# A recurrent attention and wave-mixing kernel: another order of the work, bf16 weight flips, filler matmuls at the start, and DMA transposes near the end

## The chip, the cores and the metric

One core of a Trainium2 chip runs the kernel: TensorE (PE), VectorE (DVE), ScalarE (ACT), GpSimd (POOL), the queue of SyncE (SP) that issues nearly all DMAs, and 16 DMA engines. The metric is the device time of one execution in microseconds (us). PEld is PE's loading of a stationary operand, which overlaps its matmuls.

## The reference, cut to what matters

Batch 4, 8 heads of 48, 768 tokens, so rows of 384. All inputs and the output are float32.

```python
for t in range(S):                                   # per batch and head
    cur = outer(u * k[t], v[t])
    y[t] = r[t] @ (state + cur)
    state = w[:, None] * state + outer(k[t], v[t])
x = heads of y side by side                          # (B, 768, 384)
theta = x @ w_theta
z = w_tok_r @ (x * cos(theta)) + w_tok_i @ (x * sin(theta))   # over the tokens
u = x + z
out = u + maximum(u @ w_ch, 0)
```

## The kernel before, in words

The recurrence is computed in chunks of 128 tokens: r is scaled by powers of w and k by inverse powers, so that within a chunk the result is a masked product, and between chunks a state is carried. A batch has 6 chunks, taken as 3 pairs (g = 3 x batch + pair, 12 in all). `build` describes the kernel as a list of tasks, in this order of the text:

- `setup` (L308): masks, the identity, and the tables wpow and wpinv of powers of w, which start with a load of w, a matmul on ones (L363) and exponentials on ACT.
- `heads` (L487), per batch: r scaled into Rw (L492), flipped by PE and evacuated as RT, transposed.
- `attention` (L506), per pair: k scaled into Kw (L520, f32 in, bf16 out), flipped as KT; v cast (vb); scores (L543), masked into mAT (L548); the diagonal term (PD L553, L561, dg, yd L568); state sums (L585, L593, L603, L613); outputs (L627, L632), and x (L639). Then x is flipped by PE into a bank (the helper at L473), evacuated as xT, multiplied with w_theta (theta, L651), sine and cosine are taken on ACT (L655, L658), and zr (DVE L661) and zi (POOL L664) are formed.
- `token_weights` (L445): each 128 x 768 block of the two token matrices is loaded in f32, flipped by PE in f32 against an f32 identity (6 transposes, L456, into two banks), and evacuated by ACT or DVE as bf16.
- `mixing` (L668), per pair of chunks of a batch: per chunk 24/2 = 12 matmuls of 384 columns (L683) in four parts of three, which all wait for zr and zi of all three pairs; the sum with x (un, L689); six flips of un (L473) evacuated as uT; six matmuls with w_ch (L700); relu and sum (fin, L704); one store of 384 KB (L708).

The helper `copy` (L257) is the line L259 on ACT and L261 on the others; every load is issued at L404.

`Plan.order` (L88) is a list scheduler that runs when the program is built. Every task carries for each engine that may take it a cost in ns (time on the engine, latency until others see it), data it reads and writes, PSUM banks it needs (two double banks, four single ones), and a priority. It steps through time by these costs, gives each free engine the ready task of the lowest priority number, and so fixes the order on each engine and the engine of each task. At run time every engine goes through its list in that order and waits where an operand is late. Loads have priorities near -1e6 and so go out in the order of the text when their slot (a ring of 10) is free. A `lock` keeps tasks on DVE and POOL that share a port from being planned at the same time. Until `cold` (25 us) the scheduler counts PE's costs 1.6 times.

Of the kernel before, what the change touches and what calls it, by code (L numbers as in the profile page):

```python
# [22 lines left out]
SLOTS = (2, 2, 1, 1, 1, 1)  # L23


class Task:
    __slots__ = ("opts", "fn", "deps", "prio", "seq", "acq", "uses", "nwait", "users", "ready",
                 "start", "done", "end", "mode", "lock", "eng", "name")


class Plan:
# [7 lines left out]
    cold = 25000.0  # L39
# [6 lines left out]
    def add(self, opts, fn, rd=(), wr=(), prio=0.0, acq=(), use=(), mode=0, lock=False, name=""):  # L46
        t = Task()
        t.opts, t.fn, t.prio, t.mode, t.lock, t.name = opts, fn, prio, mode, lock, name
        t.seq = len(self.tasks)
# [24 lines left out]

    def pick_banks(self, acq, free, now, kept):

        got = {}
        avail = [i for i in range(len(self.slots)) if free[i] <= now and i not in kept]
        for tok in sorted(acq, key=lambda k: -self.width[k]):
            c = [i for i in avail if self.slots[i] >= self.width[tok]]  # L80
            if not c:
                return None
            i = min(c, key=lambda i: (self.slots[i], free[i]))
            avail.remove(i)
            got[tok] = i
        return got

    def order(self):  # L88
        for t in self.tasks:
            t.users, t.nwait, t.ready = [], len(t.deps), {e: 0.0 for e in t.opts}  # L90
# [5 lines left out]
        def wake(t):  # L96
            for e in t.opts:
                waiting[e].append(t)
# [11 lines left out]
        while len(out) < n:  # L110
            for e in ENGINES:
                while free_at[e] <= now:
                    best, got = None, None
                    kept = set()
                    for t in sorted(waiting[e], key=lambda t: (t.prio, t.seq)):
                        if t.ready[e] > now or (t.lock and port > now):
                            continue
                        if len(t.opts) > 1:
                            mine = now + t.opts[e][0]
                            if any(max(free_at[o], t.ready[o], now) + t.opts[o][0] < mine  # L120
                                   for o in t.opts if o != e):
# [15 lines left out]
                    for o in t.opts:  # L137
# [5 lines left out]
                    if e == PE:  # L143
                        if t.mode != last_mode:
                            ns += 80.0
                        last_mode = t.mode
                        if now < self.cold:
                            ns *= 1.6
                    if t.lock:
# [39 lines left out]
def act_op(n, psum=True, ptr=False):  # L189
    return (n / 1.2 + (85 if psum else 100) + (90 if ptr else 0), 135)  # L190


def dve_op(n, rate=1.0):
    return (n / (0.96 * rate) + 70, 115)


def pool_op(n, rate=1.8):
    return (170 + rate * n, 100)


def pe_op(ns):
    return (ns, 215)
# [3 lines left out]
def kernel(  # L206
# [15 lines left out]
    ctx.enter_context(tc.manual_schedule())  # L222
    for t in P.order():
# [3 lines left out]
def build(ctx, tc, nc, r, k, v, w, u, moe_w_theta, moe_w_tok_r, moe_w_tok_i, moe_w_ch, out):  # L227
# [39 lines left out]
    pi2 = sb.tile([C, 1], F32, name="pi2")  # L267
    w_row = sb.tile([1, HD], F32, name="w_row")
# [39 lines left out]
    def setup():  # L308
# [6 lines left out]
        def fills(e):  # L315
            nc.vector.memset(ones, 1.0)
# [3 lines left out]
            for t in Sbs:  # L320
                nc.vector.memset(t, 0.0)
# [3 lines left out]
        P.add({DVE: (600, 100)}, fills, wr=["ones", "wu", "pi2", "uw", "bmask", "Sb0"], prio=-200)  # L325
# [81 lines left out]
    def load_r(b, parts=1):  # L407
        n = H // parts
        for i in range(parts):
            h = slice(i * n, (i + 1) * n)  # L410
            load(3500 / parts, r_fs[b % NR][:, h],
# [9 lines left out]
    def load_kv(b, pr, src):  # L421
        i = slot()
        for c in range(2):
            t0 = (2 * pr + c) * C
            load(1080, Ls[i][:, c, :, :D], src[b, :, t0:t0 + C, :].transpose([1, 0, 2]),
# [9 lines left out]
    def square(src, dst, key, prio, pos=None):  # L435
        s3 = src.rearrange("(o p) n -> p o n", p=C)
        for o, n in ((0, 2), (2, 1)):
            i = slot()
            load(560 * n, flat(i)[:, :n * HD].rearrange("p (o c) -> p o c", o=n),
# [5 lines left out]
    def token_weights(tos, prio):  # L445
        for to in tos:
            for src, dst, key in ((moe_w_tok_r, WrT, "WrT"), (moe_w_tok_i, WiT, "WiT")):
                i = slot()
                load(1100, flat(i)[:, :S], src[to * C:(to + 1) * C, :], L2(i))
                tok = ("W", key, to)  # L450

                def flip(e, i=i, tok=tok):
                    for g in range(2):
                        for j in range(3):
                            o = (3 * g + j) * C
                            nc.tensor.matmul(dbl(tok)[:, g, j * C:(j + 1) * C],  # L456
                                             flat(i)[:, o:o + C], ident_f, is_transpose=True,
                                             start=(j == 0), stop=(j == 2))
                P.add({PE: pe_op(660)}, flip, rd=L2(i) + ["ident_f"], acq=[(tok, 2)],
                      prio=prio + to, name="Wflip")  # L460

                def evac(e, tok=tok, dst=dst, to=to):
                    copy(e, dst[:, :, to * C:(to + 1) * C].rearrange("p (g j) c -> p g j c", g=2),
                         dbl(tok)[:, :, :3 * C].rearrange("p g (j c) -> p g j c", j=3))
                P.add({ACT: act_op(6 * C), DVE: dve_op(6 * C)}, evac, use=[tok],
                      wr=[(key, to)], prio=prio + to, name="Wevac")
# [17 lines left out]

    nS = [0]

    def heads(b, base):  # L487

        rf, Rw, RT = r_fs[b % NR], Rws[0], RTs[b % 2]
        for hp in range(HP):  # L490
# [5 lines left out]
            opts = {POOL: pool_op(576, 2.15)}  # L496
            if b == 0:
                opts[DVE] = dve_op(576)
            P.add(opts, scale_r, rd=[("r_f", b % NR, hp)] + [("wpow", n) for n in range(NCH)],
                  wr=[("Rw", hp)], prio=base + 0.1 * hp, lock=True, name="rscale")  # L500
# [5 lines left out]
    def attention(b, pr, base):  # L506
# [16 lines left out]
        opts = {POOL: pool_op(2 * HD, 2.15)}  # L523
        if b == 0:
            opts[DVE] = dve_op(2 * HD)
        P.add(opts, scale_k, rd=L2(ik) + [("wpinv", 0), ("wpinv", 1)], wr=[kK], prio=pb,
              lock=True, name="kscale")
# [3 lines left out]
        P.add({ACT: act_op(2 * HD, False)}, lambda e: copy(  # L531
            e, vb.rearrange("p a (h d) -> p (a h) d", h=H),
            Ls[iv][:, :, :, :D].rearrange("p a h d -> p (a h) d")),
            rd=L2(iv) + ["tables done"], wr=[kv_], prio=pb + 1, name="vcast")

        for c in range(2):
# [18 lines left out]
            rd=[kT] + rt_keys, wr=[kP], prio=pb + 2.5, lock=True, name="PD")  # L555
        td = ("dg", g)

        def diag(e):
# [9 lines left out]
        P.add({POOL: pool_op(2 * HD, 1.7)}, lambda e: nc.gpsimd.tensor_mul(  # L568
            yd.rearrange("p a (h d) -> p (a h) d", h=H), wide(dg, D),
            vb.rearrange("p a (h d) -> p (a h) d", h=H)), rd=[kd, kv_], wr=[ky], prio=pb + 3,  # L570
            lock=True, name="yd")
# [36 lines left out]
        P.add({DVE: dve_op(HD), ACT: (490, 135)}, mid,  # L608
# [10 lines left out]
        def outputs(e):  # L619
            for c in range(2):  # L620
                cc = 2 * pr + c
                first = True
                for s, keep in ((Sb_in, S_in and c == 0), (Sb_mid, c == 1)):
                    if not keep:
                        continue
# [5 lines left out]
                for h in range(H):  # L631
                    nc.tensor.matmul(dbl(ty)[:, c, h * D:(h + 1) * D], mAT[:, c, h % 2, h // 2, :],  # L632
                                     vb[:, c, h * D:(h + 1) * D], start=first,
                                     stop=(h == H - 1), skip_group_check=True)
                    first = False
        P.add({PE: pe_op(740)}, outputs, rd=rt_keys + [kM + (0,), kM + (1,), kv_, S_mid] +
              ([S_in] if S_in else []), acq=[(ty, 2)], prio=pb + 5, name="y")
# [6 lines left out]
        flips(xT, [x[:, 2 * pr + t, dk * C:(dk + 1) * C] for t in range(2) for dk in range(ND)],  # L644
              ("TX", g), pb + 6, xk, [("xT", g % 2)], "xT", ev(6 * C))
        th = ("th", g)

        def theta(e):
# [15 lines left out]
        P.add({POOL: pool_op(2 * HD, 1.9)}, lambda e: nc.gpsimd.tensor_mul(  # L664
            zi[:, 2 * pr:2 * pr + 2], x[:, 2 * pr:2 * pr + 2], sn),
            rd=xk + [("sin", g % 2)], wr=[("zi", zj, pr)], prio=pb + 8, lock=True, name="zi")

    def mixing(b, pr, base):  # L668
        x, zr, zi = xs[b % 2], zrs[b % 2], zis[b % 2]
        zj = b % 2  # L670
        zk = [("zr", zj, o) for o in range(NP)] + [("zi", zj, o) for o in range(NP)]
# [3 lines left out]
        for t in range(2):  # L675
            to = 2 * pr + t
            tm = ("mx", b, to)
            for part in range(4):
                def mix(e, tm=tm, to=to, part=part):
                    WT, z = ((WrT, zr), (WiT, zi))[part // 2]  # L680
                    for j in range(3):
                        so = 3 * (part % 2) + j
                        nc.tensor.matmul(bank(tm)[:, :HD], WT[:, so, to * C:(to + 1) * C],  # L683
                                         z[:, so], start=(part == 0 and j == 0),
                                         stop=(part == 3 and j == 2))
                P.add({PE: pe_op(490)}, mix, rd=zk + [(n, to) for n in ("WrT", "WiT")],
# [77 lines left out]
```

## Time and profile before

| What | us |
|---|---|
| median of three runs (lowest, highest) | 161.48 (159.95, 161.77) |
| the profiled execution | 159.55 |
| its span, from the first to the last instruction | 157.8 |
| busy: PE, DVE, ACT, POOL | 135.1, 110.0, 76.3, 75.6 |
| DMA | 25.00 MB in 59962 packets |

The profile's page gives the busy share of each engine and the same in 40 slices of 3.9 us, each digit a tenth; PEclk is the clock granted to TensorE, in tenths of full speed. Groups of instructions are listed by line, engine and operands with their total and mean time (mean ns of one), and the idle time ahead of them with what ended it. A matmul's own duration includes its way through the array; matmuls overlap, so what one costs is better seen in the chain of work that ended last, which gives a run of them from start to start. A waits row reads: who waited, for whom, us in total, times, longest.

### The profile page before, as it was taken

The page shows a single profiled execution, that of the slowest core. Times are in us where ns is not written, and L with a number is a line of the kernel's source. Part 1 is how long each engine was busy: PE and PEld are TensorE (multiplying, and loading weights), DVE is VectorE, ACT ScalarE, POOL GpSimd, SP SyncE. Part 2 cuts the span into 40 slices and gives each one's busy share as a digit, 9 for nine tenths or more (in the row PEclk, how much of TensorE's full clock was granted, in tenths as well). Part 3 has the DMA queues.
Part 4 walks back from the last instruction along what each step waited for, and adds up shares of the span by engine and source line. Part 5 has one row for each costly group of instructions (what it writes and reads, how often), then busy time and mean ns, then how long its engine had stood idle before and what let it go on. Part 6 is the DMA issues. An engine that isn't in the chain of part 4 may idle for free.

```text
span 157.8 us, 3653 instructions
## 1 busy us (share of the span) xinstructions
PE 135.1 (86%) x1491; PEld 94.8 (60%) x1491; DVE 110.0 (70%) x158; ACT 76.3 (48%) x119; POOL 75.6 (48%) x61
## 2 busy tenths in 40 slices
PE   4068596788899999999979969999999999999950
PEld 1056474657787676668846737668567676566620
DVE  7196798624622889996999957657996975555540
ACT  3977236348988465747943465516317354000000
POOL 7000730759796564974599976900712442100000
PEclk9999997869999999999999999999999999999996
DMA  4999999999799999999999960202200022021022
GB/s 145 266 224 187 163 265 397 368 397 344 246 165 167 149 186 205 185 166 199 330 175 230 159 102 0 103 19 82 103 1 4 0 102 103 1 100 73 27 100 100
DMA packets 59962, 25.00 MB, mean 158 GB/s; under 512 B 50473, under 2 KB 58410, under 8 KB 59946
## 3 DMA queue, kind: packets, MB, share of 16 engines
q1 hardware_dynamic: 59920, 24.78, 72.9%
q8 instruction: 11, 0.18, 0.5%
q14 instruction: 5, 0.04, 0.1%
q10 hardware_dynamic: 26, 0.00, 0.0%
HBM read 20.06 MB, written 4.72 MB: 157 GB/s over the span
## 4 chain that ended last, share of the span: by engine, by line
PE 49%; DMA 14%; DVE 11%; POOL 9%; SPq 9%; issue 3%; ACT 2%; ACTq 0%; POOLq 0%; DVEq 0%
PE bank L683 22%; DMA r_f<-in_r_dram 11%; SPq L404 8%; PE bank L473 7%; PE bank L700 6%; POOL Rw L492 5%; PE bank L456 4%; DMA ld<-in_k_dram 4%; PE bank L651 3%; POOL Kw L520 3%; DVE zr L661 2%; PE bank L543 2%; DVE PD L553 2%; DVE mAT L548 1%; DVE un L689 1%
## 5 line engine op out<-in xcount | busy, mean ns | idle before, releaser
L683 PE MATMUL bank<-zi,WiT 128*128 128x384 bf16 x144 | 29.7, 326 | 0.0
L683 PE MATMUL bank<-zr,WrT 128*128 128x384 bf16 x144 | 29.2, 326 | 0.0
L548 DVE TENSOR_TENSOR mAT<-bank,mask 128x1024 bf16<-128x1024 f32 x24 | 28.7, 1213 | 0.1
L520 POOL TENSOR_TENSOR Kw<-ld,wpinv 128x768 bf16<-128x768 f32 x10 | 18.6, 1861 | 19.8 <-DMA ld<-in_k_dram 16.8
L664 POOL TENSOR_TENSOR zi<-x,sin 128x768 bf16<-128x768 bf16 x12 | 20.6, 1715 | 15.2 <-ACT sin L655 15.2
L568 POOL TENSOR_TENSOR yd<-dg,vb 128x768 bf16<-128x768 f32 x12 | 17.6, 1472 | 21.1 <-ACT dg L259 16.3
L689 DVE TENSOR_TENSOR un<-bank,x 128x384 bf16<-128x384 f32 x24 | 13.2, 552 | 6.7 <-PE bank L683 6.7
L651 PE MATMUL bank<-Wth,xT 128*128 128x384 bf16 x72 | 15.4, 357 | 2.8 <-DVE xT L261 1.4
L492 POOL TENSOR_TENSOR Rw<-r_f,wpow 128x576 bf16<-128x576 f32 x12 | 16.5, 1405 | 2.2 <-DMA r_f<-in_r_dram 2.2
L639 DVE TENSOR_TENSOR x<-bank,yd 128x768 bf16<-128x768 f32 x12 | 11.4, 953 | 8.6 <-PE bank L632 5.1
L683 PEld LDWEIGHTS <-WiT 128*128 128x128 bf16 x144 | 12.9, 98 | 7.1
L683 PEld LDWEIGHTS <-WrT 128*128 128x128 bf16 x144 | 12.8, 97 | 7.0
L259 ACT ACTIVATE vb<-ld 128x768 bf16<-128x768 f32 x12 | 10.1, 845 | 11.8 <-DMA ld<-in_v_dram 11.3
L704 DVE SCALAR_TENSOR_TENSOR fin<-bank,un 128x768 f32<-128x768 f32 x12 | 11.5, 956 | 6.2 <-PE bank L700 6.2
L655 ACT ACTIVATE sin<-bank 128x768 bf16<-128x768 f32 x12 | 9.7, 810 | 12.0 <-PE bank L651 6.5
L259 ACT ACTIVATE RT<-bank 128x768 bf16<-128x768 bf16 x16 | 12.0, 816 | 4.7 <-PE bank L473 4.6
L700 PE MATMUL bank<-Wch,uT 128*128 128x384 bf16 x72 | 13.7, 326 | 0.7 <-DVE uT L261 0.7
L661 DVE TENSOR_TENSOR zr<-bank,x 128x768 bf16<-128x768 f32 x12 | 11.4, 950 | 2.9 <-ACT bank L658 2.9
L651 PEld LDWEIGHTS <-xT 128*128 128x128 bf16 x72 | 7.3, 104 | 8.2 <-issue 2.7
L543 PE MATMUL bank<-RT,KT 64*128 64x128 bf16 x192 | 9.8, 229 | 2.1 <-ACT KT L259 0.6
L658 ACT ACTIVATE bank<-bank,pi 128x768 f32<-128x768 f32 x12 | 10.5, 873 | 0.0
L473 PE MATMUL bank<-ident,Kw 128*128 128x128 bf16 x96 | 8.4, 241 | 1.9 <-POOL Kw L520 1.7
(79 smaller groups left out, 213.0 us busy)
## 6 DMA issues: line engine op xcount, KB each, us to landing
ld<-in_k_dram SPq DMA_DIRECT2D x24, 192.0 KB, 5.6
ld<-in_v_dram SPq DMA_DIRECT2D x24, 192.0 KB, 5.2
out_dram<-fin SPq DMA_DIRECT2D x12, 384.0 KB, 2.5
r_f<-in_r_dram SPq DMA_DIRECT2D x3, 1152.0 KB, 9.1
ld<-in_moe_w_tok_r_dram SPq DMA_DIRECT2D x6, 384.0 KB, 7.2
ld<-in_moe_w_tok_i_dram SPq DMA_DIRECT2D x6, 384.0 KB, 8.4
r_f<-in_r_dram SPq DMA_DIRECT2D x2, 576.0 KB, 4.7
ld<-in_moe_w_theta_dram SPq DMA_DIRECT2D x1, 384.0 KB, 5.0
```

What stands on the lines that cost most here:

```text
L259: nc.scalar.activation(dst, src, Act.Copy)
L473: nc.tensor.matmul(bank16(tok)[:, i * C:(i + 1) * C], s, ident, is_transpose=True, start=(i == 0), stop=(i == n - 1))
L492: eng_of[e].tensor_mul(Rw[:, :, 2 * hp:2 * hp + 2, :D].transpose([0, 2, 1, 3]), rf[:, 2 * hp:2 * hp + 2, :].rearrange("p h (n d) -> p h n ...
L520: eng_of[e].tensor_mul(Kw[:, :, :, :D].rearrange("p a h d -> p (a h) d"), Ls[ik][:, :, :, :D].rearrange("p a h d -> p (a h) d"), wpinv.rea ...
L548: P.add({DVE: dve_op(8 * C)}, lambda e, tk=tk, c=c: nc.vector.tensor_mul(mAT[:, c].rearrange("p a h t -> p (a h) t"), dbl(tk).rearrange("p ...
L568: P.add({POOL: pool_op(2 * HD, 1.7)}, lambda e: nc.gpsimd.tensor_mul(yd.rearrange("p a (h d) -> p (a h) d", h=H), wide(dg, D), vb.rearrang ...
L651: nc.tensor.matmul(dbl(th)[:, t, :HD], xT[:, ND * t + dk, :], Wth[:, dk, :], start=(dk == 0), stop=(dk == ND - 1))
L661: P.add({DVE: dve_op(2 * HD)}, lambda e: nc.vector.tensor_mul(zr[:, 2 * pr:2 * pr + 2], dbl(th)[:, :, :HD], x[:, 2 * pr:2 * pr + 2]), use= ...
L664: P.add({POOL: pool_op(2 * HD, 1.9)}, lambda e: nc.gpsimd.tensor_mul(zi[:, 2 * pr:2 * pr + 2], x[:, 2 * pr:2 * pr + 2], sn), rd=xk + [("si ...
L683: nc.tensor.matmul(bank(tm)[:, :HD], WT[:, so, to * C:(to + 1) * C], z[:, so], start=(part == 0 and j == 0), stop=(part == 3 and j == 2))
L689: P.add({DVE: dve_op(HD)}, lambda e, tm=tm, t=t, to=to: nc.vector.tensor_add(un[:, t], bank(tm)[:, :HD], x[:, to]), use=[tm], rd=[("x", zj ...
L700: nc.tensor.matmul(dbl(tf)[:, t, :HD], uT[:, ND * t + dk, :], Wch[:, dk, :], start=(dk == 0), stop=(dk == ND - 1))
```

## The change

The same arithmetic with these edits:

- **Order.** A table TUNE holds for some 700 tasks a shift of the priority and the set of engines that may take the task. `Plan.tune` applies it before `order`. The shifts, up to several thousand, are larger than the steps between priorities, so they set the order of nearly everything, of the loads among themselves too. The scheduler's costs are changed (`act_op`, `dve_op`, `pool_op`, loads, `cold` = 11 us with a factor of 1.9), and the port's lock is held only by DVE and POOL.
- **Engine choices.** Scaling of r and k may be done by DVE in every batch, the cast of v by POOL, and yd and zi by DVE, where TUNE says so.
- **Weight flips.** A new task `Wcast` turns a loaded block into bf16 inside its own slot (ACT, DVE or POOL by TUNE; for most blocks POOL), the six flips take bf16 and one bank, and the evacuation reads bf16.
- **Filler matmuls.** 110 tasks of two 128x128 bf16 matmuls on a tile of zeros, with a priority behind all others, into a bank of their own until the last of them. The clears of `setup` are split so that ones and zeros come first.
- **Outputs** (L627, L632) are one task per chunk and not per pair.
- **Mixing** is cut into six parts of two matmuls, each of which needs only zr or only zi of one pair; parts alternate between the two.
- **DMA transposes.** For the last batch xT, and for g = 6 to 10 uT, is made by one `dma_start_transpose` from SBUF to SBUF on SP's queue (`turn`), in place of six flips and an evacuation. The scheduler counts 1600 ns on SP and 2100 ns latency for it.
- **The last pair** (g = 11) is flipped, multiplied and stored one chunk at a time.

```diff
+    def tune(self, table):
+        for seq, (more, mask) in table.items():
+            t = self.tasks[seq]
+            t.prio += more
+            t.allow = tuple(e for i, e in enumerate(ENGINES) if mask >> i & 1)
...
-                        if t.ready[e] > now or (t.lock and port > now):
+                        if t.ready[e] > now or (e in t.lock and port > now):
...
+                P.add({ACT: act_op(S, False), DVE: dve_op(S, 2.0), POOL: pool_op(S, 0.9)},
+                      lambda e, i=i, half=half: copy(
+                          e, half, flat(i)[:, :S].rearrange("p (g c) -> p g c", g=2)),
+                      rd=L2(i), wr=L2(i), prio=prio + to, lock=SHARED, allow=(ACT, POOL),
+                      name="Wcast")
...
+    def turn(dst, src, prio, rd, wr, name):
+        P.add({SP: (1600, 2100)}, lambda e: nc.sync.dma_start_transpose(out=dst, in_=src),
+              rd=rd, wr=wr, prio=prio - 2e6, name=name)
...
+        if b < B - 1:
+            flips(xT, [x[:, 2 * pr + t, dk * C:(dk + 1) * C] for t in range(2)
...
+        else:
+            turn(xT, x[:, 2 * pr:2 * pr + 2].rearrange("p t n -> p (t n)"), pb + 6, xk,
+                 [("xT", g % 2)], "xT")
...
-            for part in range(4):
+            for part in range(2 * NP):
...
-                P.add({PE: pe_op(490)}, mix, rd=zk + [(n, to) for n in ("WrT", "WiT")],
+                P.add({PE: pe_op(325)}, mix, rd=[(("zr", "zi")[part % 2], zj, part // 2),
+                                                 (("WrT", "WiT")[part % 2], to)],
...
+        parts = [(0, 2)] if g < B * NP - 1 else [(0, 1), (1, 2)]
+        for lo, hi in parts:
+            n, uk, rk = hi - lo, [("un", g % 2, t) for t in range(lo, hi)], ("uT", g % 2, lo)
+            if g < B * NP // 2 or n < 2:
...
+            else:
+                turn(uT, un.rearrange("p t n -> p (t n)"), pb + 2, uk, [rk], "uT")
...
+    def warm_up():
+        for i in range(NWARM):
+            def warm(e):
+                for _ in range(2):
+                    nc.tensor.matmul(bank("warm")[:, :C], zeros, zeros, start=True, stop=True,
+                                     skip_group_check=True)
+            P.add({PE: (115, 217)}, warm, rd=["zeros"], acq=[("warm", 1)] if i == 0 else [],
+                  use=[] if i == 0 else ["warm"], wr=[] if i == 0 else ["warm"], prio=1e4 + i,
+                  name="warm")
...
     setup()
+    warm_up()
+    P.tune(TUNE)
```

More of the change, by code (lines that the diff above doesn't have):

```diff
@@ L448, in token_weights @@
                 i = slot()
-                load(1100, flat(i)[:, :S], src[to * C:(to + 1) * C, :], L2(i))
+                load(1040, flat(i)[:, :S], src[to * C:(to + 1) * C, :], L2(i))
                 tok = ("W", key, to)
[L452 to L458, printed above, removed]
```

181 lines of the change are left out of this document (98 added, 83 removed), and 123 rows, old and new, of the table TUNE.

## The prediction

> **What bounds the kernel now.** I read the page first (busy shares and the 40 slices), then the table of busy time by stretch, then the order of time on TensorE and the chain that ended last, and the groups and DMA issues for prices.
>
> ```profile
> span 157.8 us, 3653 instructions
> ...
> PE 135.1 (86%) x1491; PEld 94.8 (60%) x1491; DVE 110.0 (70%) x158; ACT 76.3 (48%) x119; POOL 75.6 (48%) x61
> ...
> PE   4068596788899999999979969999999999999950
> ...
> PEclk9999997869999999999999999999999999999996
> DMA  4999999999799999999999960202200022021022
> ```
>
> TensorE (PE) is the busiest engine, but not evenly: from the eleventh slice on its digit is almost always 9, before that it swings between 0 and 9. The end is set by a PE that is full from about 37 us on; the beginning is another stage with other limits. The table by stretch puts numbers on the two (columns: PE, PEld, DVE, ACT, POOL busy us with instruction counts, granted clock, DMA share, GB/s).
>
> ```profile
> core 0: us, PE busy (x) PEld busy (x) DVE busy (x) ACT busy (x) POOL busy (x), PEclk, DMA share, GB/s
> 8.80:37.00 28.20, 21.54 (x247) 16.24 (x248) 20.83 (x29) 14.52 (x22) 11.58 (x8) 0.88 1.21 294
> 37.00:150.50 113.50, 110.04 (x1233) 77.17 (x1233) 82.68 (x109) 55.64 (x87) 61.04 (x39) 1.00 0.63 125
> 150.50:157.80 7.30, 1.62 (x12) 0.68 (x9) 2.07 (x3) 0.00 (x0) 0.00 (x0) 0.83 0.29 105
> ```
>
> From 37.0 to 150.5 PE idles 113.50 - 110.04 = 3.5 us: there only less PE work shortens the kernel. From 8.8 (its first transposes of r, the row below) to 37.0 it idles 28.20 - 21.54 = 6.7 us, does just 247 of 1491 matmuls, and much of its busy time is a slow clock. The order of time shows that better than the clock row, whose first 25 us say 0.9 although the matmuls are slow:
>
> ```profile
> 8.81 1.44 PE L473 MATMUL bank<-ident,Rw 128*128 128x128 bf16 x12 [1.51 <-DVE Rw L492]
> ...
> 22.22 0.51 PE L473 MATMUL bank<-ident,x 128*128 128x128 bf16 x6
> ...
> 25.40 1.98 PE L651 MATMUL bank<-Wth,xT 128*128 128x384 bf16 x6 [0.63 <-DVE mAT L548]
> ...
> 32.46 2.08 PE L651 MATMUL bank<-Wth,xT 128*128 128x384 bf16 x6 [0.71 <-DVE mAT L548]
> ```
>
> Twelve transposes in 1.44 us are 0.120 us each. The chain that ended last has the full-clock prices, and the tail:
>
> ```profile
> 46.11 1.33 PE bank L456 x12
> ...
> 146.23 0.34 PE bank L473 x6
> ...
> 147.54 0.97 PE bank L700 x6
> 148.51 1.96 PE bank L683 x12
> 150.50 0.57 DVE un L689
> ...
> 151.11 0.35 PE bank L473 x3
> 151.49 0.57 DVE uT L261
> ...
> 152.11 1.16 PE bank L700 x6
> 153.29 0.96 DVE fin L704
> ```
>
> A bf16 transpose costs 0.34/6 = 0.057 us, an f32 one 1.33/12 = 0.111, a 384-column matmul 0.163. So the clock was about half from 8.8 to some 22 us, full for about 3 us (six transposes seen in 0.51), and about half again from 25.4 to 36 (six matmuls of theta seen in 1.98 and 2.08; six of the same shape pass in 0.97 later). What the clock cost is then half of the slow busy time: (21.54 - 3)/2 = 9.3 us. The first stretch thus loses 9.3 to the clock and 6.7 to waits, 16.0 us together.
>
> **The change part by part.** The sum is made against the profiled execution: span 157.8, time 159.55, so 1.75 us lie around the span. The three timed runs have a median of 161.48, 1.2% above it; the range has room for that.
>
> *f32 flips of the token weights become bf16.* 12 groups of 6; six of the 72 lie before 37 us (in the term for the start), the other 66 save 66 x (0.111 - 0.057) = 3.5 us of a full PE. Their evacuation reads bf16. New are 12 casts on ACT or POOL, by the table mostly POOL:
>
> ```profile
> L520 POOL TENSOR_TENSOR Kw<-ld,wpinv 128x768 bf16<-128x768 f32 x10 | 18.6, 1861 | 19.8 <-DMA ld<-in_k_dram 16.8
> ...
> L259 ACT ACTIVATE vb<-ld 128x768 bf16<-128x768 f32 x12 | 10.1, 845 | 11.8 <-DMA ld<-in_v_dram 11.3
> ...
> L261 DVE COPY uT<-bank 128x768 bf16<-128x768 bf16 x7 | 3.9, 556 | 3.4 <-PE bank L473 3.4
> ...
> L261 DVE CAST WrT<-bank 128x768 bf16<-128x768 f32 x2 | 1.9, 958 | 3.0 <-PE bank L456 3.0
> ```
>
> ACT's cast of the same size takes 0.85 us; POOL's is not in the trace, between 0.85 and the 1.86 of its two-input product. I take 1.2 (one input, so nearer to ACT's). Twelve at 1.2 are 14 us on an engine that has 28.20 - 11.58 = 16.6 us free in the start: hidden by PE's other work on the first batch. Without that cover the first mixing comes later by one cast, 1.2 to 1.9 us. The evacuations on DVE gain 0.4 us each, off PE's path.
>
> *Turns by DMA.* Three flips of x and five of u leave PE: 8 x 0.34 = 2.7 us. A DMA turn is not in the trace; it moves 128 x 768 x 2 bytes = 192 KB. Nearest rows:
>
> ```profile
> q1 hardware_dynamic: 59920, 24.78, 72.9%
> ...
> ld<-in_k_dram SPq DMA_DIRECT2D x24, 192.0 KB, 5.6
> ...
> out_dram<-fin SPq DMA_DIRECT2D x12, 384.0 KB, 2.5
> r_f<-in_r_dram SPq DMA_DIRECT2D x3, 1152.0 KB, 9.1
> ```
>
> The bounds are 2.5 us (the stores, in the same late stage, when the DMA slices are nearly empty) and 9.1 (the longest landing). I take 4.0, between the stores and the loads of that size, which queue. What it replaces is a flip of 0.34 and an evacuation:
>
> ```profile
> L259 ACT ACTIVATE xT<-bank 128x768 bf16<-128x768 bf16 x6 | 4.9, 810 | 5.9 <-PE bank L473 5.9
> ```
>
> that is some 1.3 us with the hand-over. So xT and uT come 2.7 us later each. Cover: mixing is now cut by pairs of rows, so while the last xT is awaited the four one-bank accumulators can take the four parts of the first two pairs, 4 x 4 x 2 x 0.163 = 5.2 us; a u turn has the next pair's mixing, 24 x 0.163 = 3.9 us. Both exceed 2.7, so I add 0. On SP the waiting turn stands before the stores and any load behind it; SP already waits for DVE's fin in front of loads:
>
> ```profile
> SPq L708 <- DVE fin L704: 60.1, 10, 14.5
> ```
>
> and the late loads were in flight until slice 23 (91 us), before batch 3's x exists. If that cover fails, a late turn costs its 2.7 us up to twice.
>
> *The tail.* The last pair goes out in halves. Behind the last mixing then stand un 0.57, three flips 0.35, an evacuation of half the columns (0.30 for 0.57), three matmuls instead of six (1.16 - 0.49 = 0.67) and half a fin (0.55 for 0.96): 0.27 + 0.49 + 0.41 = 1.2 us less. The three matmuls of the first half aren't saved, they pass under the last mixing's waits.
>
> *The start: fillers, searched order, engine choices.* 110 pairs of 128-column matmuls on zeros, lowest priority. At 0.057 to 0.120 each, all of them last 12.5 to 26.4 us. Before 8.8 us PE is nearly empty and takes, at the slow price, up to 8/0.24 = 33 pairs; the other 77 (8.7 us at the full price) fill gaps until somewhere near 25 us. Their worth lies between 0 (below nothing by a filler's 0.24 us in front of real work, now and then) and the whole 16.0 us, if the cut mixing and the new order fill the waits too. Does another engine allow it? DVE has 28.20 - 20.83 = 7.4 us free in the stretch, and can hand over what it does for POOL there:
>
> ```profile
> L492 DVE TENSOR_TENSOR Rw<-r_f,wpow 128x576 bf16<-128x576 f32 x4 | 2.8, 753 | 0.0
> ...
> L520 DVE TENSOR_TENSOR Kw<-ld,wpinv 128x768 bf16<-128x768 f32 x2 | 1.9, 952 | 0.0
> ```
>
> 7.4 + 2.8 + 1.9 = 12.1 us, more than the clock's 9.3 and less than 16.0. I take the clock's 9.3 and leave the waits as they are, since loads and DVE set most of them. The priorities of nearly all tasks move too; in the full stage that can only touch the 3.5 us of waits, which I leave.
>
> **Sum**: 157.8 - 3.5 - 2.7 - 1.2 - 9.3 = 141.1 span, + 1.75 = **142.9 us**.
>
> **The rivals.**
>
> *The clock isn't held* (or the order gains nothing early): only work and tail are saved, 142.9 + 9.3 = 152.2 us. For it: the clock fell again by 25.40 although the wait there was 0.63 us, so short waits were no safeguard; the fillers run out about there. Against it: 22.22 shows that the full clock comes with denser work, and mixing by pairs brings 384-column matmuls into that stretch. Beside this, the Trainium skill (TensorE: Matmul & The Clock Gate, Part 1) has the clock fall after a whole window of some 3.4 us idle; the 25.40 row disagrees with reading that as one gap. By the rule the fillers would be ample and the sum stays 142.9; by the row they may not be.
>
> *The waits go too*: all 16.0 us come back, 142.9 - 6.7 = 136.2 us. For it: mixing no longer waits for all three pairs. Against: DVE's 12.1 us.
>
> *Turns at the longest landing*, 9.1 us: two stand in a row at the end (last x, then the next-to-last pair's u), 2 x (9.1 - 1.3) - 5.2 - 3.9 = 6.5 us uncovered, 149.4 us. Against it: these would be 192 KB on idle queues. Beside this, the Trainium skill (VectorE: DVE Perf Modes, The three transpose paths) gives 1309 ns for a 128x128 bf16 block by DMA and 390 by TensorE, and advises TensorE where PSUM will do; six blocks in a row would be 7.9 us, an estimate from that page, and the time 147.0.
>
> *Slower*: the same place, with a turn so slow that it eats the whole 16.7 us gain: 2 x (T - 1.3) - 9.1 = 16.7 gives T = 14.2 us, from where the kernel is slower than before. It would be so if a turn goes out in small pieces: a packet took 0.729 x 157.8 us x 16 / 59920 = 0.031 us of an engine; 98,304 two-byte pieces on 16 engines would be 189 us a turn, and eight of them over 1,500 us. For it: no row shows a transposing DMA. Against: no row here shows pieces of two bytes either, and even the 1152 KB landings stay below 14.2.
>
> *Loads as the bound*: they ran to 91 us in a nearly full DMA row, and would end there again; batch 3 then needs 72 mixing matmuls (11.7 us), theta and channel (5.8 us) and some attention behind it, so that nothing before about 125 us is forced. No case of its own.
>
> **How the numbers follow.** Forecast (139 to 148 us) 0.52; waits gone too 0.18; clock not held 0.17; turns at 9.1 us 0.05; slower by turns 0.05; gains and stalls of a much denser order cancel, within 1%, 0.03. A measurement of this kernel tells about 1% from no change. Faster by over 1%: 0.92, within 1%: 0.03, slower: 0.05. The range, 136.0 to 152.5, reaches to both neighbours and leaves out the slow turns, the draw and what may lie under 136.
>
> **What would show it.** Right: about 220 more matmuls with most before 25 us; theta's first six matmuls near 1.2 us instead of 1.98; flips of weights near 0.34 per six; PE's digits 9 from about slice 7; mixing before the third pair's theta; 5.5 to 6.2 us from the last mixing to the end instead of 7.3; turns that land in 2.5 to 5.6 us. Wrong: slow matmuls again after 25 us; PE waiting for DMA turns late; PE waits over 3.5 us in the full stage, or POOL's casts as releaser of the flips.

## The result, and the profile after

The changed kernel takes 150.22 us (median of 4 runs, 148.29 to 151.17) beside 160.71 us for the kernel before in the same rounds: a ratio of 0.931, 95% interval 0.918 to 0.944. A second series on another occasion gave 149.14 beside 160.74, 0.938 (0.932 to 0.945); it is the control below. Some executions of a kernel fall in a slower state: the ratios, here and below, compare only those in the fast one, while the medians hold all of them, so that a ratio is not the quotient of its two medians. The forecast was 142.9 us: the direction is right, but of the gain of 18.6 us (from 161.48) only 10.5 came. The profiled execution took 150.43 us with a span of 148.7, so 9.1 us less span, where the sum had 16.7.

The page after (busy shares, then 40 slices of 3.7 us):

```profile
span 148.7 us, 3998 instructions
...
PE 136.0 (91%) x1663; PEld 97.7 (66%) x1663; DVE 117.5 (79%) x168; ACT 76.2 (51%) x120; POOL 65.8 (44%) x59
...
PE   4579999999978999999999979899999999999980
...
PEclk9999999999999999999999999999999999999997
DMA  4999997789999989999899999945002266736425
```

The clock row says 9 from the first slice to the tail, and PE's digits are 9 from the fourth slice but for a few 7s and 8s. By this page alone the start looks repaired. PE's busy time, though, grew by 0.9 us while its work shrank. The table by stretch (columns as in the one of before) and five rows of PE's order of time show what fills it:

```profile
8.80:37.00 28.20, 27.86 (x459) 25.00 (x457) 24.65 (x33) 19.02 (x31) 13.22 (x11) 1.00 0.98 231
37.00:143.10 106.10, 102.35 (x1176) 69.31 (x1175) 87.97 (x117) 51.34 (x79) 49.41 (x34) 1.00 0.77 164
143.10:148.70 5.60, 1.52 (x13) 0.70 (x10) 2.00 (x3) 0.87 (x2) 0.00 (x0) 0.82 0.47 170
```

```profile
8.37 0.24 PE L523 MATMUL bank<-ident_f,wu 8*128 8x8 f32 x1 [2.70 <-DMA wu<-in_u_dram]
8.54 4.45 PE L881 MATMUL bank<-zeros 128*128 128x128 bf16 x40
12.78 1.55 PE L623 MATMUL bank<-ident,Rw 128*128 128x128 bf16 x18
...
25.82 1.14 PE L807 MATMUL bank<-Wth,xT 128*128 128x384 bf16 x6
27.57 0.50 PE L607 MATMUL bank<-ident,ld 128*128 128x128 bf16 x6
```

PE stands 2.70 us at one tiny transpose until the load of u (1.5 KB) lands, and then begins with 40 fillers; the first flips of r start at 12.78, in the kernel before at 8.81. These 40 take 0.106 us each, nearly the slow price, so up to there the clock row can't be taken at its word; theta's six matmuls, at 25.82, pass in 1.14 instead of 1.98.

The fillers are not all of this delay. DVE's first Rw starts at 9.84 instead of 7.90, right behind the last table of wpow. ACT took all six of them at 4.42 before; now the last one stands behind a small operation that waits for u. What this costs at the end is not known. ACT's order of time, before and after:

```profile
4.42 3.14 ACT L370 ACTIVATE wpow<-lw_f,tok_f 128x384 f32<-128x384 f32 x6
```

```profile
8.85 0.21 ACT L529 ACTIVATE lw_p<-wup 128x4 f32<-128x4 f32 x1 [0.23 <-DVE wup L527]
...
9.20 0.60 ACT L515 ACTIVATE wpow<-lw_f,tok_f 128x384 f32<-128x384 f32 x1
```

The new parts, by groups and DMA issues:

```profile
L881 PE MATMUL bank<-zeros 128*128 128x128 bf16 x220 | 18.0, 244 | 1.9 <-DVE zeros L464 1.9
...
L401 POOL CAST ld<-ld 128x768 bf16<-128x768 f32 x7 | 5.9, 840 | 10.6 <-DMA ld<-in_moe_w_tok_r_dram 6.0
```

```profile
uT<-un SPq DMA_TRANSPOSE x5, 3.5
...
xT<-x SPq DMA_TRANSPOSE x3, 2.8
```

And the tail, in the chain that ended last:

```profile
140.54 1.62 PE bank L838 x10
142.17 0.97 PE bank L863 x6
143.14 0.18 PE bank L623 x3
...
143.35 0.50 ACT uT L399
...
143.89 1.16 PE bank L863 x6
...
145.08 0.56 DVE fin L868
```

The last mixing ends at 142.17, 6.5 us before the end; before it was 150.50 of 157.8, 7.3 us. The tail gave 0.8. The six matmuls with w_ch at 142.17 are those of the pair before the last; the six at 143.89 are both halves of the last pair, three and three, in one piece.

**A count that neither fillers nor the clock can blur.** Busy time misleads here, so I counted PE's real work: each matmul that has run by a time t, at what it takes in a run of its kind at the full clock (384 columns 0.163 us, a bf16 flip 0.057, an f32 flip 0.111, scores 0.041, outputs 0.025 and 0.043, state sums 0.043, diagonal 0.023; fillers 0). In us of work, with the kernels of the experiments below:

| by t (us) | before | after | after, again | no fillers | no table | 4 more loads | masks twice | before + fillers |
|---|---|---|---|---|---|---|---|---|
| 20 | 4.4 | 3.0 | 3.2 | 3.0 | 3.6 | 3.0 | 3.0 | 3.0 |
| 30 | 8.7 | 9.0 | 8.9 | 9.2 | 9.8 | 8.9 | 5.7 | 8.7 |
| 37 | 12.2 | 15.0 | 13.6 | 12.8 | 15.3 | 12.1 | 10.6 | 12.8 |
| 50 | 24.2 | 24.2 | 24.5 | 24.4 | 26.4 | 23.4 | 19.2 | 24.7 |
| 70 | 42.9 | 43.0 | 43.9 | 42.2 | 44.4 | 41.1 | 38.8 | 41.5 |
| 100 | 69.6 | 70.3 | 71.7 | 68.6 | 72.2 | 68.7 | 66.7 | 68.9 |
| end | 120.5 | 113.9 | 113.9 | 113.9 | 113.9 | 113.9 | 113.9 | 120.5 |

Before and after have both done 24.2 us of work at 50 us. It is not the same work: by then the kernel before has made 72 weight flips at 0.111 and 15 matmuls of mixing, the changed one 60 flips at 0.057 and 34 of mixing. So what the cheaper flips save is there; a head start beyond it is not. The kernel ends 9.1 us earlier because 6.6 us of work are gone (120.5 - 113.9), 0.8 is the tail, and the last 1.7 lie between 50 us and the end of mixing: 1.0 of them because six matmuls with w_ch now run behind the last mixing, the rest thinner gaps.

One column is one trace, and differences of about 1 us say little: by 50 us the kernel with the load of w and u first (below), whose start is nearly the same, has 25.6, and the kernels before with bf16 flips alone and with turns alone have 24.5 and 25.7, at a granted clock of 0.88 from 8.8 to 37 us.

### The profile page after: what moved, and what is told of

It is laid out like the page before. It is cut to its first block, busy times and chain, and to the rows that moved or that the text cites. A ratio compares the mean times of both kernels' runs of the same rounds, so it can differ in the third digit from the quotient of the medians.

```text
span 148.7 us, 3998 instructions
## 1 busy us (share of the span) xinstructions
PE 136.0 (91%) x1663; PEld 97.7 (66%) x1663; DVE 117.5 (79%) x168; ACT 76.2 (51%) x120; POOL 65.8 (44%) x59
## 4 chain that ended last, share of the span: by engine, by line
PE 48%; DMA 20%; DVE 16%; SPq 6%; issue 4%; POOL 2%; ACT 1%; DVEq 0%; ACTq 0%; POOLq 0%
PE bank L838 19%; SPq L549 6%; PE bank L863 6%; DVE mAT L699 5%; PE bank L623 5%; PE bank L881 5%; DMA r_f<-in_r_dram 5%; DMA ld<-in_moe_w_tok_r_dram 4%; PE bank L807 4%; DMA ld<-in_k_dram 4%; DMA wu<-in_u_dram 4%; DMA ld<-in_v_dram 4%; DVE PD L704 2%; PE bank L694 2%; PE bank L781 2%
## 5 line engine op out<-in xcount | busy, mean ns | idle before, releaser
L838 PE MATMUL bank<-zr,WrT 128*128 128x384 bf16 x144 | 34.9, 326 | 0.1
L838 PE MATMUL bank<-zi,WiT 128*128 128x384 bf16 x144 | 34.3, 326 | 0.0
L719 POOL TENSOR_TENSOR yd<-dg,vb 128x768 bf16<-128x768 f32 x9 | 13.7, 1525 | 22.7 <-ACT dg L399 17.5
L881 PE MATMUL bank<-zeros 128*128 128x128 bf16 x220 | 18.0, 244 | 1.9 <-DVE zeros L464 1.9
L881 PEld LDWEIGHTS <-zeros 128*128 128x128 bf16 x220 | 15.5, 111 | 3.2 <-DVE zeros L464 1.9
L646 POOL TENSOR_TENSOR Rw<-r_f,wpow 128x576 bf16<-128x576 f32 x8 | 12.3, 1540 | 10.7 <-ACT wpow L515 6.0
L820 POOL TENSOR_TENSOR zi<-x,sin 128x768 bf16<-128x768 bf16 x6 | 9.8, 1638 | 14.1 <-ACT sin L811 14.1
L868 DVE SCALAR_TENSOR_TENSOR fin<-bank,un 128x768 f32<-128x768 f32 (+1 forms) x13 | 11.5, 890 | 4.7 <-PE bank L863 4.7
L399 ACT ACTIVATE uT<-bank 128x768 bf16<-128x768 bf16 (+1 forms) x6 | 4.1, 704 | 16.1 <-PE bank L623 14.1
L401 POOL CAST ld<-ld 128x768 bf16<-128x768 f32 x7 | 5.9, 840 | 10.6 <-DMA ld<-in_moe_w_tok_r_dram 6.0
L814 ACT ACTIVATE bank<-bank,pi 128x768 f32<-128x768 f32 x12 | 10.5, 877 | 0.0
```

Source lines behind the costliest of these rows:

```text
L399: nc.scalar.activation(dst, src, Act.Copy)
L646: eng_of[e].tensor_mul(Rw[:, :, 2 * hp:2 * hp + 2, :D].transpose([0, 2, 1, 3]), rf[:, 2 * hp:2 * hp + 2, :].rearrange("p h (n d) -> p h n ...
L719: P.add({POOL: pool_op(2 * HD, 1.7), DVE: dve_op(2 * HD)}, lambda e: eng_of[e].tensor_mul(yd.rearrange("p a (h d) -> p (a h) d", h=H), wid ...
L868: nc.vector.scalar_tensor_tensor(fin[:, lo:hi], dbl(tf)[:, :hi - lo, :HD], 0.0, un[:, lo:hi], op0=Alu.max, op1=Alu.add), use=[tf], rd=uk, ...
L881: nc.tensor.matmul(bank("warm")[:, :C], zeros, zeros, start=True, stop=True, skip_group_check=True)
```

## The experiments

The letters in the expectations are these theories on the start. A: the loads of token weights and of the next batch, in SP's order, set what PE can have done; A2: stores that wait on SP ahead of loads delay them. B: the held clock is worth its 9.3 us, and the new order gives it back elsewhere. C: the fillers at the head, with the late load of u, push back r and all behind it. E: the chain of products on DVE sets it (Rw, Kw, masks, x, zr), and a faster PE only waits for it with fillers. Diffs are against the changed kernel where nothing else is said.

**Without fillers.**

```diff
-                for _ in range(2):
+                for _ in range(0):
```

> The changed kernel with the 110 filler tasks kept in the plan but sending no matmul, so every engine keeps its order and nothing of the result is left out. Counted at full-clock prices, both kernels had done 24.2 us of real PE work by 50 us. Theory A (supply: loads, DVE and the setup chain decide how much work PE has before 50 us, the clock little): the time stays within 1.5 us of the changed kernel's 150.2. Theory B (the held clock was worth the forecast 9.3 us and the new order gave it back): 155 to 160 us. Theory C (fillers stand ahead of the first transposes of r, which start at 12.8 us instead of 8.8): 146 to 148.5 us.

Measured: 151.98 us beside 159.54, ratio 0.955 (0.951 to 0.960). The first two stretches:

```profile
8.80:37.00 28.20, 19.74 (x245) 15.07 (x246) 24.05 (x30) 18.55 (x31) 12.20 (x10) 0.82 1.08 228
37.00:50.00 13.00, 11.89 (x152) 8.75 (x150) 10.65 (x17) 9.63 (x14) 5.47 (x5) 1.00 0.97 258
```

The granted clock falls to 0.82 in the first, PE is busy 8 us less (fillers), and the work is the same at 30 and at 50 us (at 37 it is 0.8 to 2.2 us behind). DVE's busy time in the two together is 34.7 us, with fillers 34.6. So in these traces a slow clock in the start costs nothing by 50 us. The kernel is still 1.7% behind the control, just outside A's range and well short of B's; the work column loses it from 50 to 100 us. One place is seen: zi on DVE now falls beside a product of POOL. The order of time of DVE and of POOL without fillers, then of DVE with them:

```profile
64.63 1.76 DVE L820 TENSOR_TENSOR zi<-x,sin 128x768 bf16<-128x768 bf16 x1
```

```profile
64.31 1.67 POOL L646 TENSOR_TENSOR Rw<-r_f,wpow 128x576 bf16<-128x576 f32 x1 [1.64 <-PE bank L736]
```

```profile
65.04 0.55 DVE L820 TENSOR_TENSOR zi<-x,sin 128x768 bf16<-128x768 bf16 x1
```

That is 1.2 of about 2.7 us; the rest was not followed.

**Without the fillers at the head** (20 of the 110 tasks).

```diff
-                for _ in range(2):
+                for _ in range(0 if 9 <= i < 29 else 2):
```

> The changed kernel without the 40 filler matmuls that stand on PE between the transpose of w and u (8.37 us) and the first transposes of r (12.8 us); the other 180 stay, every order is kept. Theory A: first transposes of r near 10.6 us, but 149.5 to 150.5 in the end. Theory C: 147 to 148.5 us. Theory B: the clock falls once more in the first 25 us and part of the loss comes back, 151 to 154 us.

Measured: 152.71 us, 0.961 (0.955 to 0.967), 24.4 us of work by 50 us. The first flips of r start 1.8 us earlier, at 11.0, and the operands of mixing behind them do not (first zr at 30.52, with the fillers 30.10). C falls. The kernel is 2.3% behind the control, some 3.6 us: outside the ranges of A and C and inside B's, but not for B's reason, since the granted clock is 1.00 in the first stretch too:

```profile
8.80:37.00 28.20, 24.87 (x417) 21.85 (x417) 25.09 (x33) 19.54 (x32) 12.68 (x11) 1.00 1.07 233
```

Its zi is slow at the same place as without any filler:

```profile
64.61 1.76 DVE L820 TENSOR_TENSOR zi<-x,sin 128x768 bf16<-128x768 bf16 x1
```

These two kernels are the cleanest pair on the clock: 0.82 without fillers, 1.00 with 180 of them (theta's second six take 2.08 us and 1.14), and 0.955 against 0.961 of the time. What sets both behind the control is therefore not the clock. Beyond the 1.2 us of zi, which starts 0.3 to 0.4 us behind POOL's Rw here and ahead of it in the control, it was not followed.

**Without the table.**

```diff
-    P.tune(TUNE)
```

> The changed kernel without the table of priorities and engines: the scheduler orders by the priorities of the text; bf16 flips, fillers, cut mixing, DMA turns and halves stay. Theory A: the removed PE work (6.2 us) and the tail (0.8) are there without the table, and the supply before 50 us is about the same: 149 to 153 us. Theory B (the order gave back what the clock won): 140 to 145 us. Rival D (the table carries the gain): above 156 us.

Measured: 149.06 us, 0.938 (0.934 to 0.943), as the control: the 700 shifts and engine sets are worth nothing that can be measured here. This order is 1.9 to 2.2 us ahead by 50 us, 0.5 to 1.9 by 100 us, and no longer ahead at the end.

**The load of w and u first on its queue.**

```diff
+            nc.vector.memset(wu, 0.5)
             nc.scalar.dma_start(out=w_row, in_=w.rearrange("(o h) d -> o (h d)", o=1))
+            nc.scalar.dma_start(out=wu[:HP, :, :D], in_=w.rearrange("(a b) d -> a b d", b=2))
+            nc.scalar.dma_start(out=wu[HP:, :, :D], in_=u.rearrange("(a b) d -> a b d", b=2))
```

> The changed kernel with the small loads of w and u for the transpose on PE (now issued at 2.0 and 2.8 us, landed at 8.2) issued right behind that of the row of w, so that PE doesn't stand at that transpose with 40 fillers behind it, and ACT's last power tables don't wait behind it either. Theory A: first transposes of r some 2 us earlier, time 148.5 to 150.5 us. Theory C: 146 to 148 us.

Measured: 149.67 us, 0.940 (0.935 to 0.946), and a miss: the load of u was issued third on ScalarE's queue as before, at 2.68 us instead of 2.78, and wu was still there only at 8.4. The edit did not remove the wait that it was for, and says nothing about its price.

**The changed kernel again**, and then three kernels that are the kernel before with one part of the change each.

> The changed kernel itself, beside the runs of the kernel before on one chip, for a ratio to hold the others against. Every theory: 0.92 to 0.945 of before.

Measured: 149.14 us, 0.938 (0.932 to 0.945), span 147.4.

The kernel before with the bf16 weight flips:

```diff
+                P.add({ACT: act_op(S, False), POOL: pool_op(S, 0.9)},
+                      lambda e, i=i, half=half: copy(
+                          e, half, flat(i)[:, :S].rearrange("p (g c) -> p g c", g=2)),
+                      rd=L2(i), wr=L2(i), prio=prio + to, name="Wcast")
...
-                P.add({PE: pe_op(660)}, flip, rd=L2(i) + ["ident_f"], acq=[(tok, 2)],
+                P.add({PE: pe_op(340)}, flip, rd=L2(i) + ["ident"], acq=[(tok, 1)],
```

> The kernel before with only the bf16 flips of the token weights (cast on ACT or POOL by the old scheduler, one bank, bf16 evacuation). Forecast's step (66 flips of the full stage save 3.5 us of PE): ratio to before 0.975 to 0.98. Theory A (the start is set by loads and DVE, later stages by PE work): the same, 0.97 to 0.98. Rival (the cast puts a hand-over in front of each flip and the first mixing is late): 0.99 to 1.01.

Measured: 156.78 us, 0.986 (0.976 to 0.995): 2.3 us gained of 3.9 us less work, between the forecast's range and the rival's. The chain that ended last shows where some went:

```profile
66.09 0.97 DVE fin L708
67.07 0.56 SPq L712
67.69 0.47 SPq L404
68.25 0.77 SPq L404
69.07 4.92 DMA ld<-in_v_dram
...
74.78 1.79 DVE PD L557
```

A store that waits for fin stands on SP ahead of the loads of k and v, and the next pair waits for v.

The kernel before with the eight turns:

```diff
+            turn(xT, x[:, 2 * pr:2 * pr + 2].rearrange("p t n -> p (t n)"), pb + 6, xk,
...
+            turn(uT, un.rearrange("p t n -> p (t n)"), pb + 2,
```

> The kernel before with only the eight turns by DMA (x of the last batch, u of g = 6 to 10). Forecast's step: 2.7 us of PE work gone, latency covered, ratio 0.98 to 0.985. Rival (without the cut mixing the last batch's mixing waits for all three pairs, so the last turn's 2.8 to 3.5 us landing instead of 1.3 stands open, and the turns wait on SP): 0.99 to 1.005.

Measured: 156.14 us, 0.979 (0.970 to 0.989); a turn lands after 2.8 us (x) and 3.3 (u). The 2.7 us of replaced PE work are enough to explain it.

The kernel before with the 110 filler tasks and a tile of zeros:

```diff
+    warm_up()
```

> The kernel before with only the 110 filler tasks (and the clear of their tile). Theory B (a held clock is worth the 9.3 us of the forecast): 0.94 to 0.95. Theory A (before 50 us loads, DVE and the setup decide, the fillers win little and stand in front of real work at places): 0.985 to 1.01.

Measured: 160.35 us, 1.010 (1.004 to 1.017). The same two stretches:

```profile
8.80:37.00 28.20, 24.23 (x388) 21.29 (x386) 24.01 (x29) 15.33 (x28) 11.70 (x8) 0.94 1.09 285
37.00:50.00 13.00, 13.00 (x130) 11.53 (x129) 4.28 (x5) 11.35 (x17) 12.16 (x9) 1.00 1.08 253
```

The clock rises from 0.88 to 0.94 in the first, and the work by 50 us from 24.2 to 24.7, not by anything near 9.3. Theta takes 1.15 us here (at 26.55), but the first flips of r stand behind 41 fillers and start at 11.72, so this run has the gain of the clock and the delay by fillers in one. With the pair above, B falls: a held clock is worth nothing here that the time shows.

**Stores behind later loads on SP**, each behind up to four, with the table and without.

```diff
-    for t in P.order():
+    todo = P.order()
+    for t in [t for t in todo if t.name == "out"]:
+        i = todo.index(t)
+        j, n = i + 1, 0
+        while j < len(todo) and t not in todo[j].deps and n < 4:
+            n += todo[j].name == "load"
+            j += 1
...
+    for t in todo:
```

> The changed kernel with each store put on SP behind up to four later loads, nothing else moved; its chain of waits goes at 61.6 us through fin, the store on SP, the loads behind it and a landing of 5.5 us. Theory A2 (from 50 us on PE's remaining losses come from loads that stand behind a waiting store): 1 to 2.5 us less than the changed kernel, ratio to before 0.922 to 0.932. Theory A (after 50 us only PE work counts): 0.933 to 0.943. Rival: the later store holds fin's buffer and costs, above 0.945.

> The changed kernel without the table and with each store behind up to four later loads. Without the table alone it was at 0.938 of before. Theory A2: 0.922 to 0.932, the best so far. Theory A: 0.934 to 0.942.

Measured: 150.34 us, 0.943 (0.937 to 0.949), and 149.23 us, 0.938 (0.934 to 0.941). Neither moves. A2 falls for the changed kernel. The first of the two has the slow zi too (1.76 us, at 64.84), so that row alone does not put a kernel 2% behind.

**Four more loads among the token weights.** Four extra loads of 384 KB, into tiles still unused. They are issued from 21.72 to 23.6 us, ahead of all weight blocks but two (20.86 and 21.30), and not ahead of all as was meant.

```diff
+            if more:
+                for f in fins:
+                    nc.sync.dma_start(out=f, in_=moe_w_tok_r[:C].rearrange(
+                        "p (a c) -> p a c", a=2))
+                for z in (zrs[1], zis[1]):
...
```

> The changed kernel with four extra loads of token weight blocks, 1.6 MB together, into tiles that are overwritten before they are used, just ahead of the first block of the token weights (issued at 21 us); nothing is left out of the result. At the 390 GB/s of the fast stretches they take 4.1 us. Theory A (the loads set how much work PE has before 50 us): the real PE work by 50 us is 3 to 4 us less and the time 3 to 4 us longer, ratio 0.957 to 0.965. Rival E (DVE's chain or the setup sets the start and loads have slack): at most 1 us longer, 0.935 to 0.945.

Measured: 152.18 us, 0.946 (0.937 to 0.956), beside the control's 0.938: about 1.3 us for 4.1 us of loading, but the ratio rests on two executions and its interval overlaps the control's, so a loss is not shown. The work is 1.5 to 2.9 us behind at 37 us, where the control's two traces differ by 1.4, and 0.8 to 1.1 at 50. A's 3 to 4 us (0.957 to 0.965) are outside the interval; whether the loads cost a little or nothing stays open.

**Batch 0's masks twice.** The six products with the mask in batch 0 on DVE are done twice in a row.

```diff
-            P.add({DVE: dve_op(8 * C)}, lambda e, tk=tk, c=c: nc.vector.tensor_mul(
+            P.add({DVE: dve_op(8 * C)}, lambda e, tk=tk, c=c: [nc.vector.tensor_mul(
...
+                for _ in range(2 if g < NP else 1)],
```

> The changed kernel with one edit: in the three pairs of batch 0 the multiplication of the scores by the mask (mAT on DVE, 1.21 us for one) is done twice in a row, six more of them, 7.3 us more of DVE ahead of about 45 us. The order is the same and the result complete. Both kernels have done 24.2 us of PE's real work by 50 us; with four more loads (4.1 us of loading) the changed kernel lost some 1.3 us. Theory E (DVE's chain of Rw, Kw, masks, PD, x and zr sets what PE can have done by 50 us; DVE idles only 3 to 4 us in 8.8 to 30): most of the 7.3 us come back at the end, less the 2 us that lie in DVE's gaps: +4 to +7 us, a ratio to the kernel before of 0.965 to 0.985, and 17 to 20 us of real work by 50 us. Theory A (the loads of weights and of batch 1 set it, DVE's chain has cover): at most +2 us, 0.938 to 0.950, work by 50 us 23 us or more.

Measured: 155.03 us beside 160.34, 0.974 (0.967 to 0.981): 5.7 us by the ratios (0.974 - 0.938 of 160.3), 5.0 by the spans (152.4 - 147.4), for 7.3 us more of DVE. The ratio and the 19.2 us of work by 50 us are inside E's ranges and outside A's. DVE's order of time, the three zr of batch 0 in the kernel before, after, and with the masks twice:

```profile
29.86 0.95 DVE L661 TENSOR_TENSOR zr<-bank,x 128x768 bf16<-128x768 f32 x1
...
36.83 0.95 DVE L661 TENSOR_TENSOR zr<-bank,x 128x768 bf16<-128x768 f32 x1
...
41.94 0.96 DVE L661 TENSOR_TENSOR zr<-bank,x 128x768 bf16<-128x768 f32 x1
```

```profile
30.10 0.96 DVE L817 TENSOR_TENSOR zr<-bank,x 128x768 bf16<-128x768 f32 x1
...
37.19 0.95 DVE L817 TENSOR_TENSOR zr<-bank,x 128x768 bf16<-128x768 f32 x1
...
43.01 0.94 DVE L817 TENSOR_TENSOR zr<-bank,x 128x768 bf16<-128x768 f32 x1
```

```profile
35.22 0.95 DVE L818 TENSOR_TENSOR zr<-bank,x 128x768 bf16<-128x768 f32 x1
...
44.31 0.95 DVE L818 TENSOR_TENSOR zr<-bank,x 128x768 bf16<-128x768 f32 x1
...
48.77 0.96 DVE L818 TENSOR_TENSOR zr<-bank,x 128x768 bf16<-128x768 f32 x1 [0.21 <-ACT bank L815]
```

The operands of the first batch's mixing come no earlier after the change than before it (30, 37 and 43 us), and 5 to 7 us later as soon as DVE has 7.3 us more to do. Some 70 to 80% of what is put on DVE comes out at the end. E holds for the changed kernel, in this direction: that less work on DVE would shorten it is not shown, nor was the kernel before tried in this way.

## Why the prediction was right or wrong, point by point

**The step that failed: the start.** The prediction put it so: "I take the clock's 9.3 and leave the waits as they are, since loads and DVE set most of them." By its own sum the start brought 157.8 - 148.7 - 3.5 - 2.7 - 0.8 = 2.1 us in place of 9.3, and the work by 50 us says that not even those lay in the start. The clock was held, theta took 1.14, the weight flips 0.50 as the rows print six of them (x at 22.22 printed 0.51 before, so the full price), all as forecast; only the conclusion failed. Half of the slow busy time is a gain only where PE sets the pace. From 8.8 to 37 us it did not: at twice the clock PE is done sooner and waits for its operand, or runs a filler. Fillers on the kernel before (1.010), the pair without fillers and without the head fillers (0.955 at a clock of 0.82, 0.961 at 1.00) and the masks twice (-5.0 us by 50 us) show this from three sides. The operands say it too: from DVE's first Rw to the last zr of batch 0 it takes 31.4 to 34.2 us in the eight traces with fillers and neither more loads nor more masks (granted clock 0.94 or 1.00 in this stretch), and 32.3 to 34.0 in the four without fillers (0.82 or 0.88). That is 0.6 us between the means, less than the traces of either kind differ by.

The sign was in the rows shown. DVE was busy 20.83 of 28.20 us, and I read the other 7.4 as room that a faster PE could use, and added 4.7 that DVE "can hand over" to POOL. The change went the other way: on DVE stand three Rw of batch 1 and two zi of batch 0, which were POOL's work before. DVE's rows after:

```profile
9.84 3.30 DVE L646 TENSOR_TENSOR Rw<-r_f,wpow 128x576 bf16<-128x576 f32 x3
...
16.34 0.69 DVE L401 COPY KT<-bank 128x1024 bf16<-128x1024 bf16 x1 [2.34 <-PE bank L623]
...
39.30 3.32 DVE L646 TENSOR_TENSOR Rw<-r_f,wpow 128x576 bf16<-128x576 f32 x3 [1.16 <-DMA r_f<-in_r_dram]
42.54 0.54 DVE L820 TENSOR_TENSOR zi<-x,sin 128x768 bf16<-128x768 bf16 x1
```

The last zr of batch 0 at 43.01 stands behind batch 1's Rw, which first waits 1.16 us for r: 4.5 us in front of the operand that mixing needs. DVE's busy time from 8.8 to 50 us rose from 25.99 (20.83 + 5.16 in the kernel before) to 34.59 (24.65 + 9.94), for the same 24.2 us of PE work. The order without the table has 2.2 us more work by then and still no shorter time, so the start is perhaps worth little by itself even where it is better; what an order with a shorter DVE chain would bring was not tried.

Nearly all signs that the prediction named for a right start came true (fillers before 25 us, theta near 1.2, digits of 9, mixing before the third theta): they watch PE, and none watches when an operand is ready.

*Rivals.* "The clock isn't held (or the order gains nothing early)", 152.2 us, is the one whose second half came true; its first did not, the clock was held from about 14 us (12 fillers at 14.18 take 0.056 us each). That the range reaches to 152.5, and so holds the result, is owed to this rival and not to the mechanism of the forecast. The 149.4 us of late turns lie nearest to the result, by chance: no turn was that late. Waits going too (136.2) would have needed DVE's operands earlier, and they came no earlier. "Loads as the bound ... No case of its own" stays open: four more loads gave 1.3 us, which is inside the noise. The Trainium skill (TensorE: Matmul & The Clock Gate, Part 1) has the clock fall after an idle window of some 3.4 us. The profile with fillers agrees, with 1.00 granted from there to 143.1 us; whether a held clock shortens this kernel is another question, and it did not.

**The weight flips** (3.5 us late): PE's work fell by 3.9 with the six early ones, as counted. Alone they gave 2.3 us, an interval of 0.8 to 3.8, with one store in front of loads visible in the chain; in the changed kernel the work is gone from a PE that is nearly full. The casts took 0.84 us on POOL where I took 1.2, and PE's flips waited for them once, for 0.4 us.

**The turns** (2.7 us): right. Alone 3.3 us, 1.8 to 4.9. I took 4.0 for the landing between 2.5 and 9.1; 2.8 to 3.5 were measured. The Trainium skill (VectorE: DVE Perf Modes, The three transpose paths) has 1309 ns for a 128x128 block, from which I had estimated 7.9 us for six; the measurement decides, 0.5 to 0.6 us a block in a turn of six.

**The tail** (1.2 us): 0.8. The first half's three matmuls were to "pass under the last mixing's waits". DVE's and PE's order of time show why they don't:

```profile
141.57 1.19 DVE L846 TENSOR_TENSOR un<-bank,x 128x384 bf16<-128x384 f32 x2
...
142.98 0.50 PE L623 MATMUL bank<-ident,un 128*128 128x128 bf16 x6
...
143.89 1.15 PE L863 MATMUL bank<-Wch,uT 128*128 128x384 bf16 x6 [0.41 <-ACT uT L399]
144.59 1.04 DVE L868 SCALAR_TENSOR_TENSOR fin<-bank,un 128x384 f32<-128x384 f32 x2 [0.45 <-PE bank L863]
```

Both un come back to back behind the end of mixing, so the halves are flipped and multiplied together, and the six matmuls of the pair before, whose uT is a turn, stand in front of them for 0.97 us.

**The full stage**: PE idles 106.10 - 102.35 = 3.75 us from 37.0 to 143.1 against 3.5 before; leaving that term alone was right.

## What to carry to other kernels

A slow clock costs time only on an engine that sets the pace: before halving its busy time, ask what its next operand waits for, and whether that would come sooner. Count work at full-clock prices against time, without fillers; busy shares and clock digits go to 9 without one operand more. To find which engine carries a stage, double one of its operations and see how much of it arrives at the end: here 5.0 to 5.7 of 7.3 us for DVE, and for the loads 1.3 of 4.1, which the noise covers.

## What the runs showed of the hardware

A product on DVE with two inputs in SBUF is slowed while POOL works: zi takes 0.55 us alone and 1.76 beside POOL's Rw (rows above). PD takes 0.69 alone, at 64.02 in the kernel without fillers, and took 1.79 at 74.78 in the kernel with bf16 flips alone, where POOL made a Kw from 74.19 to 76.01. Three Rw took 3.30 us at 9.84, 1.10 each, with one of POOL's own Rw beside them (9.88, 1.97 us), while the mean of one in the kernel before is 0.75. The Trainium skill (GPSIMD Engine Reference, Specifications) names this contention; the factor of three is from here.

A load of 1.5 KB for u, issued at 2.78 us, is awaited until 8.37 us, beside the bulk loads on SP's queue.
